# K weights loaded first, three loads on ScalarE's queue, two duplicate tiles dropped, more dummy matmuls, new instruction orders

## Chip, cores and metric

One core of one Trainium2 chip. The metric is device microseconds for one execution, lower is better. The core's engines work in parallel and each executes its own instruction list in order: TensorE (PE, matmuls and PE transposes), VectorE (DVE), ScalarE (ACT), GpSimd (POOL), and SyncE (SP), which only issues DMAs here.

## The reference, cut to what matters

```
x = A_x                                   # 1 x 2048 x 448, bf16
n = layernorm(x)
q, k, v = split(n @ A_wqkv)               # 16 heads of 28
pq, pk = phi(q), phi(k)                   # phi(t) = t+1 if t>0 else exp(t), + 1e-6
kv, z = pk^T v, sum_s pk                  # per head: linear attention
h = x + ((pq kv) / (pq z)) @ A_wo
m = layernorm(h)
out = h + (gelu(m @ B_w_gate) * (m @ B_w_up)) @ B_w_down     # 448 -> 1792 -> 448
```

## The kernel before, in words

The 2048 rows are 16 tiles of 128 rows. There are three stages, and they overlap.

Stage 1 (K stage): for each tile, VectorE takes the statistics (`bnst1`, `bnag1`: L427, L428), ScalarE makes 1/std (L434, L436), and VectorE or GpSimd writes the normalized tile `xnn` (L467, L473, L497, L500). It must be transposed to be a matmul operand. Tiles 0 to 3 are transposed on TensorE (`tr_t`, L485) and copied out of PSUM by ScalarE and VectorE (`evxA_t`, `evxD_t`: L492, L494); tiles 4 to 15 by DMA transposes (`xT`, L504). `K0 Q0 Q1 K1` are single-tile projections (L525, four matmuls each, 128 rows deep); the others work on pairs of tiles (`K2K3` and so on, L544) as two half programs `a` and `b` of 6 and 8 matmuls, each 64 rows deep, which run two at a time. phi of k is an Exp on ScalarE (`ek`, L561) and two VectorE operations (`ck`, `pk`: L562, L564). `pk` reads PSUM too, so the bank comes free after it. `pt` (L579) accumulates n^T pk over all tiles in four PSUM banks. The pairs of projections use four further banks, two at a time, so a pair waits for the `pk` of two pairs before.

Stage 2 (hinge): from the finished `pt` come z (L607, L608) and the small matrices `kv` and `w2` (L620, L636). Then tile by tile: `t1`, `dr`, `rd`, `pn` (L671, L675, L678, L680: the normalized attention weights), transposed on TensorE for tiles 0 and 1 (`tro`, L697; copies `evo`) or by a DMA for later pairs (`oT`, L708). `out` (L722 for tiles 0 and 1; L737 for pairs, halves `outa`, `outb`) gives the attention output, `hr` (L744) adds x, and the second layer norm (L427 to L440) writes `hn` (L757 on VectorE for tiles 0 and 1, L760 on GpSimd). The projections `Q4Q5` to `Q14Q15` are spread over this time. `hn` is kept twice side by side, 896 wide, so that seven 128-column transposes yield both halves in the row positions that the next stage needs. For tiles 0 and 1 GpSimd writes the second copy (`dupP_t`, L763), and TensorE transposes all seven blocks (`trh_t`, L777), which ScalarE and VectorE copy out (`evh`). Later tiles are duplicated by VectorE (`wrap`) and transposed by DMA (`hT`, L790).

Stage 3 (feed-forward): `gu` (L856 and L858, gate and up, 64 rows deep, two at a time), Gelu on ScalarE (`ge`, L881), product on VectorE (`hm`, L883), and `down` (L808, L826) in chunks of 2, 2, 4, 4 and 4 tiles; `gu2_v` is a step of the first two chunks, `gu4_v` of the last three. `outa`, `outb` of later pairs stand between them.

What sets the order: `ORDERS` is a table of task numbers for each engine, written out in advance; `_Graph.place` reads it. The waits are worked out from what tasks read and write; `HOLD` only sorts a task's waits. `LOADS` says which queue issues which input load and in what order; a string such as `sp:wqk` loads the first 384 rows of the q and k columns at once, `wqka` and `wqkb` the last 64 rows to the lower and the upper half of the partitions. The `WARM` dummy matmuls (L422) on a tile of ones come first on TensorE.

Of the kernel before, what the change touches and what calls it, by code (L numbers as in the profile page):

```python
# [7 lines left out]
ALU = mybir.AluOpType  # L8
# [36 lines left out]
)  # L45
HOLD = {
# [182 lines left out]
def bass_sequential_preLN__linear_attn_block__glu_gated_geglu__prompt_kernel(  # L229
# [14 lines left out]
    HT_SINGLE = (1,)  # L244
    B1_CHUNKS = [2, 2, 4, 4, 4]
    WARM = 40
# [4 lines left out]
    DUP_POOL = (0, 1)  # L251
    K_SINGLE = (0, 14)
    WIDE = (0, 1, 2)
    LOADS = "sp:x0 act:x1 sp:x2-3 sp:wqk sp:wqka sp:wqkb sp:x4-7 sp:x8-11 sp:x12-15"
# [4 lines left out]
    with es:  # L259
# [108 lines left out]
        def dma_w(q, name):  # L368
            kinds = "".join(k for k in "QK" if k.lower() in name[1:3])
            c0, c1 = ("Q" not in kinds) * D, (1 + ("K" in kinds)) * D  # L370
            if name[-1] in "ab":
                i = "ab".index(name[-1])
                dma(q, wqk_sb[HALF[i], 3, c0:c1], A_wqkv[384:448, c0:c1], [b_w[k][1 + i] for k in kinds], "d" + name)
            else:
                dma(q, wqk_sb[:, 0:3, c0:c1], rows3(A_wqkv, c0, c1), [b_w[k][0] for k in kinds], "d" + name)
# [48 lines left out]
        G.add("pe", warm_fn, r=[b_ones], w=[b_ps[3]], name="warm")  # L424

# [237 lines left out]
        def a2_pair(p):  # L663
# [90 lines left out]
            for t in (a, a + 1):  # L754
# [7 lines left out]
                if t in DUP_POOL:  # L762
                    op("pool", lambda e, t=t, sh=sh: e.tensor_scalar(hn[:, sh, D:2 * D], x_sb[:, t, :], mv2[:, t, 0:1], rs2[:, t:t + 1], ALU.subtract, ALU.mult),  # L763
                       [b_x[t], b_mv2[t], b_rs2[t]], [b_hnd[sh]], "dupP_%d" % t)
                elif p == 0 or p in HT_SINGLE:
# [4 lines left out]
                if p == 0:  # L770
                    banks = BK_TH[t]

                    def ftrh(e, sh=sh, banks=banks):
                        ins = None
                        for k in (0, 1, 2, 4, 5, 6, 3):
# [111 lines left out]
        for chunk, nt in enumerate(B1_CHUNKS):  # L887
# [6 lines left out]
            for t in range(t0 - t0 % 2, t0 + nt - 1, 2):  # L894
                if t < T - 2:
                    b2_pair(t)
                else:
                    b2_tile(t)
                    b2_tile(t + 1)
            t0 += nt  # L900

        G.place(ORDERS)
        G.finalize(nc, es)

# [48 lines left out]
```

## Time and profile before

| | |
|---|---|
| time, median of 3 runs | 198.53 us (197.41 to 199.61) |
| the profiled execution's own time | 200.15 us |
| its span | 198.3 us, 1.85 us less than its own time |
| TensorE matmuls busy | 187.8 us (95%) |
| VectorE, ScalarE, GpSimd busy | 126.3, 71.9, 57.7 us |
| granted TensorE clock, mean | 0.991 |

The profile is of one execution. It lists busy time by engine, the busy share in 40 slices of the span (4.96 us each), the chain of work that ended last, and the groups of instructions. The trace behind it gives each instruction with its start, its duration and, in brackets, the idle time of its engine just before it and what ended that. A "PE ... x12" row covers twelve matmuls that follow each other.

### The profile page before, as it was taken

How to read it: one execution, taken by the hardware profiler on the slowest of the kernel's cores; microseconds unless marked ns; L12 is line 12 of the kernel's file. 1: busy time of each engine (PE TensorE's matmuls, PEld its weight loads, DVE VectorE, ACT ScalarE, POOL GpSimd, SP SyncE). 2: the span in 40 equal slices, each digit the busy share in tenths (PEclk: the TensorE clock that was granted, in tenths of full speed). 3: DMA queues.
4: the chain of work that ended last, by engine and by line, in shares of the span. 5: the costliest groups of instructions: out<-in, count | busy, mean ns of one | idle time of the engine just before them, and what ended most of it. 6: DMA issues, size and time to landing. Idle time of an engine off the chain costs nothing.

```text
span 198.3 us, 4730 instructions
## 1 busy us (share of the span) xinstructions
PE 187.8 (95%) x2002; PEld 101.5 (51%) x2002; DVE 126.3 (64%) x261; ACT 71.9 (36%) x162; POOL 57.7 (29%) x105
## 2 busy tenths in 40 slices
PE   7799999999499989999999999999999999999993
PEld 7343445554158857785444444444444444444452
DVE  2669988799859975998659764564454241545231
ACT  3467634199745411331223322323223211243100
POOL 3237970154825541954223300004500000000000
PEclk9999999999969999999999999999999999999999
DMA  5982558995590092308701164010054010100003
GB/s 140 317 264 53 107 111 186 223 219 120 112 311 10 1 148 53 56 3 166 171 3 34 24 120 111 3 46 0 3 99 90 0 46 3 46 0 3 0 26 117
DMA packets 34693, 17.59 MB, mean 89 GB/s; under 512 B 27376, under 2 KB 33392, under 8 KB 34672
## 3 DMA queue, kind: packets, MB, share of 16 engines
q1 hardware_dynamic: 34528, 17.18, 38.1%
q8 instruction: 16, 0.26, 0.5%
q10 hardware_dynamic: 144, 0.11, 0.3%
q14 instruction: 5, 0.04, 0.1%
HBM read 8.37 MB, written 1.84 MB: 51 GB/s over the span
## 4 chain that ended last, share of the span: by engine, by line
PE 79%; DVE 11%; DMA 6%; issue 1%; POOL 1%; ACT 1%; SPq 0%
PE ps L858 37%; PE ps L808 17%; PE ps L737 6%; PE ps L544 5%; PE ps L579 5%; DMA wqk_sb<-in_A_wqkv_dram 3%; PE ps L525 3%; PE ps L826 3%; DVE st L427 3%; DMA pqnT<-pqn 2%; DVE hh L883 1%; DVE pk L564 1%; PE ps L856 1%; DVE e L562 1%; DVE mv L428 1%
## 5 line engine op out<-in xcount | busy, mean ns | idle before, releaser
L858 PE MATMUL ps<-hnT,wgu_sb 64*128 64x512 bf16 (+1 forms) x490 | 88.3, 333 | 0.0
L856 PE MATMUL ps<-hnT,wgu_sb 64*128 64x512 bf16 (+1 forms) x490 | 88.2, 333 | 0.0
L881 ACT ACTIVATE gl<-ps 128x256 bf16<-128x256 f32 (+1 forms) x84 | 35.2, 453 | 88.5 <-PE ps L856 86.8
L883 DVE TENSOR_TENSOR hh<-ps,gl 128x256 bf16<-128x256 f32 (+1 forms) x84 | 40.5, 507 | 39.7 <-ACT gl L881 39.7
L858 PEld LDWEIGHTS ps<-hnT,wgu_sb 64*128 64x128 bf16 x490 | 45.7, 94 | 34.1
L856 PEld LDWEIGHTS ps<-hnT,wgu_sb 64*128 64x128 bf16 x490 | 45.8, 94 | 3.0 <-issue 0.5
L808 PE MATMUL ps<-wd_sb,hh 64*128 64x448 bf16 x392 | 39.5, 349 | 0.0
L808 PEld LDWEIGHTS ps<-wd_sb,hh 64*128 64x128 bf16 x392 | 19.8, 94 | 17.6 <-issue 0.4
L671 POOL TENSOR_TENSOR t<-pq,zbc 128x448 f32<-128x448 bf16 x15 | 16.7, 1129 | 26.0 <-DVE zbc L608 10.3
L544 PE MATMUL ps<-wqk_sb,hh 64*128 64x448 bf16 x196 | 22.9, 350 | 0.5 <-DVE pk L564 0.4
L427 DVE BATCH_NORM_STATS2 st<-x_sb 128x6 f32<-128x448 bf16 x32 | 18.9, 610 | 3.6 <-DMA x_sb<-in_A_x_dram 3.5
L579 PE MATMUL ps<-pk,xnn 64*128 64x448 bf16 x128 | 14.8, 349 | 0.3 <-DVE pk L564 0.3
L544 PEld LDWEIGHTS ps<-wqk_sb,hh 64*128 64x128 bf16 x196 | 8.7, 95 | 10.2 <-PE ps L544 1.4
L813 DVE TENSOR_TENSOR x_sb<-ps,x_sb 128x896 bf16<-128x896 f32 x7 | 7.6, 1085 | 7.2 <-PE ps L808 7.2
L439 POOL TENSOR_SCALAR ln<-mv 128x2 f32<-128x2 f32 x7 | 2.0, 280 | 31.0 <-DVE mv L428 31.0
L737 PE MATMUL ps<-w2p,pqnT 64*128 64x448 bf16 x84 | 9.9, 349 | 0.9 <-DMA pqnT<-pqn 0.9
L561 ACT ACTIVATE e<-ps 128x896 bf16<-128x896 f32 (+1 forms) x10 | 7.5, 764 | 8.2 <-PE ps L544 5.5
L744 DVE TENSOR_TENSOR x_sb<-ps,x_sb 128x896 bf16<-128x896 f32 (+1 forms) x9 | 8.8, 982 | 2.3 <-PE ps L737 2.3
L760 POOL TENSOR_SCALAR hn<-x_sb,nm,rs 128x448 bf16<-128x448 bf16 x14 | 10.0, 718 | 0.6
L579 PEld LDWEIGHTS ps<-pk,xnn 64*128 64x128 bf16 x128 | 6.1, 94 | 6.7 <-DVE pk L564 1.2
L675 DVE TENSOR_REDUCE den<-t 128x32 f32<-128x896 f32 (+1 forms) x9 | 8.7, 969 | 0.4 <-POOL t L671 0.3
L564 DVE SCALAR_TENSOR_TENSOR pk<-ps,e 128x896 bf16<-128x896 f32 (+1 forms) x10 | 8.8, 892 | 0.1
(84 smaller groups left out, 153.3 us busy)
## 6 DMA issues: line engine op xcount, KB each, us to landing
wd_sb<-in_B_w_down_dram SPq DMA_DIRECT2D x1, 1568.0 KB, 7.8
out_dram<-x_sb SPq DMA_DIRECT2D x7, 224.0 KB, 2.2
x_sb<-in_A_x_dram SPq DMA_DIRECT2D x3, 448.0 KB, 7.2
wgu_sb<-in_B_w_gate_dram SPq DMA_DIRECT2D x1, 896.0 KB, 11.9
wgu_sb<-in_B_w_up_dram SPq DMA_DIRECT2D x1, 896.0 KB, 15.3
wqk_sb<-in_A_wqkv_dram SPq DMA_DIRECT2D x1, 672.0 KB, 6.5
wgu_sb<-in_B_w_gate_dram SPq DMA_DIRECT2D x1, 672.0 KB, 6.0
wgu_sb<-in_B_w_up_dram SPq DMA_DIRECT2D x1, 672.0 KB, 8.4
```

What stands on the lines that cost most here:

```text
L427: op("dve", lambda e: e.bn_stats(st[:, t, :], src_ap), [b_src], [b_st[t]], "bnst%s_%d" % (tag, t))
L544: ins = e.matmul(ps[:, bk0 + i_, 0:D], xnT[HALF[h], t, c, :], wqk_sb[HALF[h], c, c0:c0 + D], start=(part == "a" and c == 0), stop=(c == 3))
L564: op("dve", lambda e: e.scalar_tensor_tensor(pk[:, ip:ip + n, :], psK, EPS, e1[:, i:i + n, :], ALU.max, ALU.add), b_ps[bu:bu + n] + b_e1[i ...
L579: ins = e.matmul(ps[:, BK_PT[c], 0:D], xnn[HALF[h], t // 2, tcols(t, c)], pk[HALF[h], t % PK_R, :], start=(t == 0 and o == 0), stop=(t == ...
L671: op(eng, lambda e, t=t, n=n: e.tensor_tensor(t1[:, n, :], pq[:, t, :], zbc[:, :], ALU.mult), [b_pq[t]] + b_z, [b_t1[n]], "t1%s_%d" % (eng ...
L737: ins = e.matmul(ps[:, BK_OUT[n], 0:D], pqnT[rows, i2, n, g, :], w[rows, g, :], start=(g == 0 and s == 0), stop=(g == 3 and s == 1))
L760: op("pool", lambda e, t=t, sh=sh: e.tensor_scalar(hn[:, sh, 0:D], x_sb[:, t, :], nm2[:, t:t + 1], rs2[:, t:t + 1], ALU.add, ALU.mult), [b ...
L808: ins = e.matmul(ps[:, BK_O[n], 0:D], hh[HALF[h], j, (t % HR) * 128:(t % HR + 1) * 128], wd_sb[HALF[h], j, :], start=(s == 0 and j == 0), ...
L856: first = e.matmul(psG[:, jj * N:(jj + 1) * N], wgu_sb[A_, k, j * 128:(j + 1) * 128], hnT[A_, r0:r0 + nt, ka_, :], start=(k == 0), stop=(k ...
L858: ins = e.matmul(psU[:, jj * N:(jj + 1) * N], wgu_sb[B_, k, j * 128:(j + 1) * 128], hnT[B_, r0:r0 + nt, kb_, :], start=(k == 0), stop=(k = ...
L881: G.add("act", lambda e, gi=gi, cs_=cs_, psG=psG: e.activation(gl[:, gi, cs_], psG[:, cs_], AF.Gelu_apprx_tanh), r=[b_ps[BK_G[i]]], w=b_gl ...
L883: op("dve", lambda e, dst=dst, srcU=srcU, srcL=srcL: e.tensor_tensor(dst, srcU, srcL, ALU.mult), [b_ps[BK_U[i]]] + b_glh, [b_ar[j_][t % HR ...
```

## The change

Five things are changed.

- Loads. The 384 rows of q and k columns, one load of 672 KB before, become two, `wk` first and `wq` after it (336 KB each). The tails become one load that reads the 64 rows twice (`wqkt`). x of tiles 2 and 3 and the tails are issued by ScalarE instead of SyncE, ahead of its table load.
- The second copy of `hn` for tiles 0 and 1 (`dupP`, GpSimd) is left out. `trh` now makes six of its seven blocks from the one copy, and the block that wraps round from four transposes of 64 columns: 16 transposes for 14.
- 43 dummy matmuls for 40 at the start, and a new group of 7 (`fill_0`), placed after `tr_0`.
- All five orders in `ORDERS` are new, and `HOLD` with them.
- On GpSimd the constants are written in another order.

```
-    LOADS = "sp:x0 act:x1 sp:x2-3 sp:wqk sp:wqka sp:wqkb sp:x4-7 sp:x8-11 sp:x12-15"
+    LOADS = "sp:x0 act:x1 sp:wk act:x2-3 act:wqkt sp:wq sp:x4-7 sp:x8-11 sp:x12-15"
-    WARM = 40
+    WARM = 43
+    FILL = (7,)
-    DUP_POOL = (0, 1)
...
+            if name[-1] == "t":
+                src = A_wqkv[384:448, c0:c1].unsqueeze(0).to_broadcast([2, 64, c1 - c0])
+                dma(q, wqk_sb[:, 3, c0:c1], src, [b_w[k][i] for k in kinds for i in (1, 2)], "d" + name)
...
-                if t in DUP_POOL:
-                    op("pool", lambda e, t=t, sh=sh: e.tensor_scalar(hn[:, sh, D:2 * D], ...), ..., "dupP_%d" % t)
-                elif p == 0 or p in HT_SINGLE:
+                if p == 0:
+                    pass
+                elif p in HT_SINGLE:
...
-                        for k in (0, 1, 2, 4, 5, 6, 3):
+                        for k in (0, 1, 2, 4, 5, 6):
                             for h in range(2):
-                                ins = e.transpose(..., hn[HALF[h], sh, k * 128:(k + 1) * 128], ident[HALF[h], HALF[h]])
+                                c0 = k * 128 - (k > 3) * D
+                                ins = e.transpose(..., hn[HALF[h], sh, c0:c0 + 128], ident[HALF[h], HALF[h]])
+                        for r_, c0 in enumerate((384, 0)):
+                            for h in range(2):
+                                ins = e.transpose(psb[HALF[r_], banks[h], 192:256], hn[HALF[h], sh, c0:c0 + 64], ident[HALF[h], HALF[h]])
...
+        for i, n in enumerate(FILL):
+            G.add("pe", fill(n), r=[b_ones], w=[], name="fill_%d" % i)
```

In ORDERS one line of the five engines' tables, TensorE's first, shows what the rows are: numbers of tasks.

```
-    "31 38 47 55 66 63 70 85 73 88 89 81 82 97 77 98 78 83 84 79 116 80 117 93 95 94 136 96 137 121 156 123 157 124"
+    "31 38 754 66 47 55 70 63 73 85 88 77 89 81 78 82 97 79 83 98 84 80 116 117 95 93 96 136 94 137 121 156 123 157"
```

Three places show how the instructions move. In the changed file the lines stand a little lower: L422 is L425 there, L485 is L496, L525 is L536, L544 is L555, L697 is L708, L722 is L733, L737 is L748, L777 is L788 with L791, and the dummies of `fill_0` are L433.

The first place is SyncE at the program's start, the input loads; before:

```order
L355 DMA x_sb<-in_A_x_dram 128x448
L355 DMA x_sb<-in_A_x_dram 128x896
L355 DMA wqk_sb<-in_A_wqkv_dram 128x3x896
L355 DMA wqk_sb<-in_A_wqkv_dram 64x896 x2
L355 DMA x_sb<-in_A_x_dram 128x1792 x3
```

and now SyncE's first rows, followed by ScalarE's own first rows in a second piece:

```order
L355 DMA x_sb<-in_A_x_dram 128x448
L355 DMA wqk_sb<-in_A_wqkv_dram 128x3x448 x2
L355 DMA x_sb<-in_A_x_dram 128x1792 x3
L355 DMA wv_sb<-in_A_wqkv_dram 128x3x448
L355 DMA wv_sb<-in_A_wqkv_dram 64x448
```

```order
L355 DMA x_sb<-in_A_x_dram 128x448
L355 DMA x_sb<-in_A_x_dram 128x896
L355 DMA wqk_sb<-in_A_wqkv_dram 128x1x896
L414 ACT_TABLE_LOAD
L445 ACTIVATE ln<-mv,eps_t 128x1
```

The k columns have moved from behind x of tiles 2 and 3 to second place on SyncE; x of tiles 2 and 3 and the tails stand on ScalarE, ahead of its table load.

The second place is TensorE at the start: dummies, `tr`, the single projections and the first pairs; before, then now:

```order
L422 MATMUL ps<-ones_bf 128x128 x40
L485 MATMUL ps<-ident,xnn 128x64 x24
L525 MATMUL ps<-wqk_sb,hh 128x448 x4
L485 MATMUL ps<-ident,xnn 128x64 x8
L525 MATMUL ps<-wqk_sb,hh 128x448 x12
L544 MATMUL ps<-wqk_sb,hh 128x448 x14
```

```order
L425 MATMUL ps<-ones_bf 128x128 x43
L496 MATMUL ps<-ident,xnn 128x64 x8
L433 MATMUL ps<-ones_bf 128x128 x7
L536 MATMUL ps<-wqk_sb,hh 128x448 x4
L496 MATMUL ps<-ident,xnn 128x64 x16
L536 MATMUL ps<-wqk_sb,hh 128x448 x4
L496 MATMUL ps<-ident,xnn 128x64 x8
L536 MATMUL ps<-wqk_sb,hh 128x448 x8
L555 MATMUL ps<-wqk_sb,hh 128x448 x6
```

Three `tr` stood ahead of K0, now one does, with seven dummies behind it; `tr_1`, `tr_2` follow K0, and the last eight single-tile matmuls are K1 then Q1 (Q1 then K1 before).

The third place is TensorE at the hinge, from the second `tro` to the first `gu`; before, then now:

```order
L697 MATMUL ps<-ident,pqn 112x64 x8
L544 MATMUL ps<-wqk_sb,hh 128x448 x8
L722 MATMUL ps<-w,pqnT 128x448 x4
L544 MATMUL ps<-wqk_sb,hh 128x448 x6
L722 MATMUL ps<-w,pqnT 128x448 x4
L544 MATMUL ps<-wqk_sb,hh 128x448 x14
L777 MATMUL ps<-ident,hn 128x64 x14
L544 MATMUL ps<-wqk_sb,hh 128x448 x8
L737 MATMUL ps<-w,pqnT 128x448 x8
L777 MATMUL ps<-ident,hn 128x64 x14
L737 MATMUL ps<-w,pqnT 128x448 x8
L856 MATMUL ps<-hnT,wgu_sb 128x256
```

```order
L733 MATMUL ps<-w,pqnT 128x448 x4
L708 MATMUL ps<-ident,pqn 112x64 x8
L555 MATMUL ps<-wqk_sb,hh 128x448 x6
L733 MATMUL ps<-w,pqnT 128x448 x4
L555 MATMUL ps<-wqk_sb,hh 128x448 x22
L788 MATMUL ps<-ident,hn 128x64 x12
L791 MATMUL ps<-ident,hn 64x64 x4
L788 MATMUL ps<-ident,hn 128x64 x12
L791 MATMUL ps<-ident,hn 64x64 x4
L870 MATMUL ps<-hnT,wgu_sb 128x256
```

`outa_1` and `outb_1` (L737) have left the stretch ahead of the first `gu`: they now stand behind `gu2_2` and `gu2_3`. All projections stand ahead of both `trh`. On SyncE, `oT_1` is now issued after the fifth of the eight copies of `w2`, and `oT_3` ahead of `hT_2` and `hT_3`.

More of the change, by code (lines that the diff above doesn't have):

```diff
@@ L370, in dma_w @@
             c0, c1 = ("Q" not in kinds) * D, (1 + ("K" in kinds)) * D
-            if name[-1] in "ab":
+            if name[-1] == "t":
+                src = A_wqkv[384:448, c0:c1].unsqueeze(0).to_broadcast([2, 64, c1 - c0])
+                dma(q, wqk_sb[:, 3, c0:c1], src, [b_w[k][i] for k in kinds for i in (1, 2)], "d" + name)
+            elif name[-1] in "ab":
                 i = "ab".index(name[-1])
@@ L424, in bass_sequential_preLN__linear_attn_block__glu_gated_geglu__prompt_kernel, with fill, fn @@
         G.add("pe", warm_fn, r=[b_ones], w=[b_ps[3]], name="warm")
+        def fill(n):
+            def fn(e):
+                ins = None
+                for _ in range(n):
+                    ins = e.matmul(ps[:, 3, 0:128], ones_bf[:], ones_bf[:], start=True, stop=True)
+                return ins
+            return fn
         def ln_stats(t, src_ap, b_src, st, mv, b_st, b_mv, tag):
@@ L761, in a2_pair @@
                        [b_x[t], b_nm2[t], b_rs2[t]], [b_hn[sh], b_hnd[sh]], "nhP_%d" % t)
-                if t in DUP_POOL:
-                    op("pool", lambda e, t=t, sh=sh: e.tensor_scalar(hn[:, sh, D:2 * D], x_sb[:, t, :], mv2[:, t, 0:1], rs2[:, t:t + 1], ALU.subtract, ALU.mult),
-                       [b_x[t], b_mv2[t], b_rs2[t]], [b_hnd[sh]], "dupP_%d" % t)
-                elif p == 0 or p in HT_SINGLE:
+                if p == 0:
+                    pass
+                elif p in HT_SINGLE:
                     op("dve", lambda e, sh=sh: e.tensor_copy(hn[:, sh, D:2 * D], hn[:, sh, 0:D]), [b_hn[sh]], [b_hnd[sh]], "wrap1_%d" % t)
@@ L774, in ftrh @@
                         ins = None
-                        for k in (0, 1, 2, 4, 5, 6, 3):
+                        for k in (0, 1, 2, 4, 5, 6):
                             for h in range(2):
-                                ins = e.transpose(psb[:, banks[h], k * 64:(k + 1) * 64], hn[HALF[h], sh, k * 128:(k + 1) * 128], ident[HALF[h], HALF[h]])
+                                c0 = k * 128 - (k > 3) * D
+                                ins = e.transpose(psb[:, banks[h], k * 64:(k + 1) * 64], hn[HALF[h], sh, c0:c0 + 128], ident[HALF[h], HALF[h]])
+                        for r_, c0 in enumerate((384, 0)):
+                            for h in range(2):
+                                ins = e.transpose(psb[HALF[r_], banks[h], 192:256], hn[HALF[h], sh, c0:c0 + 64], ident[HALF[h], HALF[h]])
                         return ins
-                    G.add("pe", ftrh, r=[b_hn[sh], b_hnd[sh], b_ident], w=[b_ps[b] for b in banks], name="trh_%d" % t)
+                    G.add("pe", ftrh, r=[b_hn[sh], b_ident], w=[b_ps[b] for b in banks], name="trh_%d" % t)
                     for h, eng in enumerate(("act", "dve")):
```

78 rows, old and new, of tables (HOLD, ORDERS) are left out of this document.

## The prediction

> **What bounds the kernel now.** I read the chain by engine first, then busy time in chosen windows, then the instructions in order of time where TensorE is not full.
>
> ```profile
> PE 79%; DVE 11%; DMA 6%; issue 1%; POOL 1%; ACT 1%; SPq 0%
> ```
>
> ```profile
> core 0: us, PE busy (x) PEld busy (x) DVE busy (x) ACT busy (x) POOL busy (x), PEclk, DMA share, GB/s
> 14.40:24.15 9.75, 8.98 (x89) 3.76 (x89) 8.98 (x21) 6.75 (x16) 8.27 (x21) 1.00 0.41 81
> 24.15:37.70 13.55, 13.55 (x142) 6.80 (x144) 10.89 (x21) 4.91 (x8) 4.28 (x8) 1.00 0.78 158
> 50.80:54.80 4.00, 1.14 (x24) 0.51 (x22) 3.54 (x8) 3.06 (x6) 3.24 (x2) 1.00 0.63 122
> 54.80:58.20 3.40, 3.38 (x32) 1.59 (x34) 1.24 (x4) 1.28 (x2) 0.00 (x0) 0.50 1.02 337
> 58.20:72.00 13.80, 13.66 (x226) 11.60 (x222) 12.76 (x24) 6.28 (x12) 8.87 (x12) 1.00 0.32 53
> 95.00:195.00 100.00, 100.00 (x958) 48.56 (x954) 48.99 (x104) 27.01 (x71) 10.62 (x21) 1.00 0.18 39
> ```
>
> In each row the second number is TensorE's busy time and the third from the end the granted clock. TensorE is full from 95 to 195 us, and the change touches no matmul there; what it can win lies ahead, where TensorE idles or is slow (at full clock a 64-row matmul of 448 columns takes 13.55 / 142 = 0.095 us, as two run at a time): the start, the hinge (idle for 2.86 us of 50.8 to 54.8, then 3.40 us at granted clock 0.50) and a short wait near 72 us. Time won there reaches the end, because nothing behind has slack to swallow it except new waits.
>
> **Start.** The rows of TensorE and VectorE in order of time:
>
> ```profile
> 1.26 4.45 PE L422 MATMUL ps<-ones_bf 128*128 128x128 bf16 x40 [1.26 <-POOL ones_bf L388]
> ...
> 6.64 0.28 DVE L494 COPY hh<-ps 128x256 bf16<-128x256 bf16 x1
> ...
> 8.31 1.67 PE L525 MATMUL ps<-wqk_sb,hh 128*128 128x448 bf16 x4 [0.56 <-DMA wqk_sb<-in_A_wqkv_dram]
> ...
> 10.24 4.20 PE L525 MATMUL ps<-wqk_sb,hh 128*128 128x448 bf16 x12
> 10.35 0.29 DVE L494 COPY hh<-ps 128x256 bf16<-128x256 bf16 x1 [1.70 <-PE ps L485]
> ...
> 10.78 1.15 DVE L427 BATCH_NORM_STATS2 st<-x_sb 128x6 f32<-128x448 bf16 x2
> ...
> 15.05 0.42 DVE L562 TENSOR_SCALAR e<-e 128x448 bf16<-128x448 bf16 x1 [1.34 <-ACT e L561]
> ```
>
> K0 has its transposed tile at 6.92 and waits for weights until 8.31. The twelve matmuls of Q0, Q1, K1 take 4.20 us, 0.35 each. VectorE waits 1.70 us for the late `tr_3` and 1.34 us for the Exp of K1, which stands last of the four. From 14.4 to 24.15 VectorE is busy 8.98 of 9.75 us: it sets the pace there, since each `pk` frees the banks of a later pair. So only a VectorE that runs earlier makes this stage earlier.
>
> When would the K weights be there? The loads:
>
> ```profile
> 0.00:4.00 4.00, 2.74 (x26) 2.75 (x27) 0.55 (x1) 1.28 (x1) 1.82 (x12) 1.00 0.46 128
> 4.00:5.40 1.40, 1.40 (x16) 1.40 (x14) 1.33 (x5) 0.81 (x4) 0.44 (x1) 1.00 0.77 218
> 5.40:8.30 2.90, 1.49 (x27) 0.75 (x25) 2.36 (x10) 1.72 (x7) 0.89 (x4) 1.00 1.00 294
> ```
>
> ```profile
> wqk_sb<-in_A_wqkv_dram SPq DMA_DIRECT2D x1, 672.0 KB, 6.5
> ```
>
> By time these rows moved 0.51 MB by 4.0 us, 0.82 by 5.4, 1.67 by 8.3. x of tiles 0 to 3 is 0.46 MB (448 KB for four tiles), the old q and k load 0.69: that count is reached near 6.5, and K0 started at 8.31, so landing trails the count by up to 1.8 us. Now 0.80 MB stand up to `wk`, reached at 5.4, and 1.03 with the tails, at 6.1: landed at 5.4 to 7.9. K0 then starts between 6.95 and 7.9; I take 7.1. `wq` lands by 9.1 and x of tiles 4 to 7 at the same byte count as before, so between 8.9 (at the last row's rate) and the 10.78 at which it is first read.
>
> The Trainium skill (DMA: Bandwidth & Descriptors, "Issuing engines are not separate DMA queues") speaks against the move to ScalarE: both queues feed the same 16 engines, and a second issuer saves only time to issue. The trace neither shows nor excludes it, as only one load was ScalarE's. By it the order of bytes alone would help, which is how I counted.
>
> The new dummies: 43 x 0.111 (4.45 / 40) end at 6.03 for 5.71, and seven more take 0.78 us while `evx` of tile 0 copies out, up to 6.92: hidden, with at most the 0.3 us of the three on the path. ScalarE's two more issues take some 0.4 us each,
>
> ```profile
> 0.79 0.38 ACTq L355 DMA_DIRECT2D x_sb<-in_A_x_dram  x1
> ```
>
> and stand ahead of a table load and of work that waits for VectorE's first statistics in any case: nothing, and 0.8 us if that cover were gone.
>
> So VectorE: `tr_1`, `tr_2` come after K0 now, three `evx` and `ck` of tile 0 near 9.1 instead of about 10.6, right behind the 10.35 row; then statistics of tiles 4 and 5 at 9.1 to 10.8; K1 ahead of Q1 removes the 1.34 us. Sum: 1.34 + (0 to 1.7), of which I take 0.3, because the loads hold the first statistics: **1.6 us earlier**. The bounds are 0 (the loads or GpSimd's tiles, busy 8.27 of 9.75, hold everything) and 3.0 (both waits go). Should the projections run faster than 0.35 behind the dummies, that adds nothing beyond these bounds, as VectorE sets the pace.
>
> **Hinge.** From the first `hr` to the last wait ahead of `gu`:
>
> ```profile
> 48.00 0.62 DVE L744 TENSOR_TENSOR x_sb<-ps,x_sb 128x448 bf16<-128x448 f32 x1
> ...
> 48.65 0.63 DVE L427 BATCH_NORM_STATS2 st<-x_sb 128x6 f32<-128x448 bf16 x1
> ...
> 49.31 0.18 DVE L428 BATCH_NORM_AGGREGATE mv<-st 128x2 f32<-128x6 f32 x1
> ...
> 49.53 0.29 ACT L434 ACTIVATE ln<-mv,eps_t 128x1 f32<-128x1 f32 x1 [0.34 <-DVE mv L428]
> 49.86 0.20 ACT L436 ACTIVATE rs<-ln 128x1 f32<-128x1 f32 x1
> 50.09 0.40 DVE L757 TENSOR_SCALAR hn<-x_sb,mv,rs 128x448 bf16<-128x448 bf16 x1
> 50.16 3.88 POOL L763 TENSOR_SCALAR hn<-x_sb,mv,rs 128x448 bf16<-128x448 bf16 x2 [0.18 <-ACT rs L436]
> 50.28 0.92 ACT L588 ACTIVATE pq<-ps 128x896 bf16<-128x896 f32 x1 [0.22 <-PE ps L544]
> ...
> 52.22 0.38 PE L777 MATMUL ps<-ident,hn 64*128 64x64 bf16 x14 [1.41 <-DVE den L675]
> 52.43 0.92 PE L544 MATMUL ps<-wqk_sb,hh 64*128 64x448 bf16 x8
> 52.63 0.54 ACT L784 ACTIVATE hnT<-ps 128x448 bf16<-128x448 bf16 x1 [0.83 <-PE ps L777]
> ...
> 54.82 1.67 PE L737 MATMUL ps<-w,pqnT 64*128 64x448 bf16 x8 [1.47 <-DVE pq L667]
> ```
>
> GpSimd's duplicates take 1.94 us each; the first ends at 52.1, and `trh_1` starts at 52.22, although `hn` of its tile was ready at 50.49. The 1.41 us end with it (the bracket names a VectorE operation that merely ended then). The 1.47 us ahead of `outa_1` end too, since it leaves this stretch. What is late next? From the end of the second `out1`, tile 1 needs 0.62 + 0.63 + 0.18 + 0.29 + 0.20 + 0.40 = 2.3 us to its `hn`, then 0.38 for `trh` and 0.54 for the copy: 3.2 us to `gu`. TensorE has 22 projection matmuls in that time (0.095 each, 2.1 us) and two `trh` of 0.4: at least 0.3 us idle. ScalarE's copies of the projections, 0.92 each, stand ahead of `ln` and of the copy, so up to 1.8 more; and a `tro` may wait 0.6 for VectorE's copy of `w2` (as wide as the `hr` of 0.62) and the second `out1` 0.3 for its operand, both behind such work. I take 2.2 of a range of 0.3 to 3.9 against 2.86 now: **0.7 us won**, bounds 2.6 won and 1.0 lost. The two extra transposes for each `trh` cost 0.05 each at most, inside that.
>
> The half clock is the larger part: 32 matmuls in 54.8 to 58.2 took 3.4 us where full clock takes 1.7. It follows a stretch of the same length with TensorE a third busy, and did not follow the one before:
>
> ```profile
> 47.97:51.40 3.43, 2.83 (x24) 1.01 (x20) 3.27 (x9) 2.76 (x6) 3.25 (x3) 1.00 0.25 69
> 51.40:54.80 3.40, 1.13 (x22) 0.51 (x22) 2.97 (x6) 2.54 (x5) 2.64 (x2) 1.00 0.70 132
> ```
>
> With some 1.6 us idle together, a window of 3.4 is half busy, which lies between the 33% that lost the clock and the 83% that kept it, and the worst idle is broken by `trh_0`: I take it as kept, **1.7 us won** in the profiled execution, bounds 0 and 1.7.
>
> **Near 72 us.** `outa_2` waits 0.85 us for its DMA transpose.
>
> ```profile
> 72.71 0.74 PE L737 MATMUL ps<-w2p,pqnT 64*128 64x448 bf16 x6 [0.85 <-DMA pqnT<-pqn]
> ```
>
> ```profile
> hnT<-hn SPq DMA_TRANSPOSE x8, 4.1
> ```
>
> The Gelus of two `gu2` stand 1.53 us apart, and VectorE's `pn` and `hm` take this long to the next start:
>
> ```profile
> 61.44 0.60 ACT L881 ACTIVATE gl<-ps 128x512 bf16<-128x512 f32 x1 [0.93 <-PE ps L856]
> 62.97 0.60 ACT L881 ACTIVATE gl<-ps 128x512 bf16<-128x512 f32 x1 [0.93 <-PE ps L856]
> ```
>
> ```profile
> 64.20 1.09 DVE L685 TENSOR_TENSOR pqn<-pq,rd 128x896 bf16<-128x896 bf16 x1
> 65.22 0.68 DVE L883 TENSOR_TENSOR hh<-ps,gl 128x512 bf16<-128x512 f32 x1
> ```
>
> From `gu2_0` to `gu2_7` TensorE now does 7 `gu2` of 1.53, 44 matmuls of `out` and 56 of `down` at 0.095: 10.7 + 4.2 + 5.3 = 20.2 us. VectorE, from the same point to the duplicate of tile 3, has seven products of 0.6, eight operations as wide as `pn` (three `pn`, three `dr`, two `hr`) of 1.02, three statistics of 0.6 and small ones of some 2.8: 17.0 us; the transpose takes 4.1: 21.1. So the old 0.85 us goes and about 0.9 returns ahead of `gu2_7`: **0**, bounds 0.85 won and 2.5 lost, if VectorE also stalls as it does at 92% of 58.2 to 72. Behind that TensorE has more work queued than the transposes need; the end (last `down`, add, store) has the same operations, so nothing.
>
> **The sum.** 1.6 + 0.7 + 1.7 + 0 = 4.0 us off the profiled execution's 200.15 gives 196.15, its span 198.3 to 194.3. That execution is slower than all three runs shown, median 198.53. One profile cannot tell how often the clock loss comes, and runs 0.5 to 2.7 us shorter speak against its coming in all of them, so I count half of it against the median: 198.53 - 1.6 - 0.7 - 0.85 = **195.4 us**.
>
> **Rivals.**
>
> First, the loads hold the start. Then its term is 0: 198.53 - 0.7 - 0.85 = 197.0. For it: x of tiles 4 to 7 has the same bytes ahead as before. Against: the 1.34 us behind K1 are no load's. Chance 0.12.
>
> Second, the clock falls to a half in the changed hinge as well, so nothing of that term is won: 198.53 - 1.6 - 0.7 = 196.2, and if the median runs had kept full clock until now, 0.85 worse, 197.1. For it: about 1.6 us idle around two short `trh`; against: half busy is not a third. The Trainium skill (TensorE: Matmul & The Clock Gate, "Part 1: The HAM clock gate") says that a free-running window of some 3.4 us decides, so that the same idle time costs in one execution and not in the next. The trace agrees as far as one execution can: the slow stretch is 3.40 us long. By the same rule the seven dummies should bring full clock to K0; the trace has 40 dummies at 0.111 us without a speed-up. Chance 0.15.
>
> Third, the wait ahead of `gu2_7` eats the gain: VectorE reaches the duplicate of tile 3 about 2.5 us late, 195.4 + 2.5 = 197.9. Chance 0.12.
>
> Fourth, slower: narrow rows. The weights now come in rows of half the length, and twice as many. If a load takes its time by the row, `wk` takes 6.5 us as the whole did, from its issue near 1.2 to 7.7, and `wq` behind it until 14.2; Q0 then starts at 14.2 for 10.24, and x of tiles 4 to 7 waits too. That adds 4.0, less the 1.55 of the hinge: 201.0. It decides from the point where `wq` lands later than about 11.8, where the loss passes the hinge's gain. Against: x of tiles 0 and 1 has rows of this length and the first 4 us moved 0.51 MB although they begin with nothing moving. Chance 0.08.
>
> **Chances and range.** The forecast has 0.53. A measurement here can tell about 1%, so faster means below 196.5. The forecast counts as faster, the second rival half so, and a little of the first and third: 0.64. Same: the rest of those three, 0.27. Slower, above 200.5: the narrow rows and a little of the third: 0.09. The likeliest case alone spans 193.5 to 197; with the upper bounds of the start and hinge terms it reaches down to 192.8, with the third rival up to 198.8, and what lies beyond is the slower case and a little on each side.
>
> **What would show it.** Right: K0 near 7.1 us and K1's Exp ahead of Q1; `ck` of the second tile near 13.2 for 15.05; no GpSimd `hn` row of 1.94 us, and `gu2_0` near 53 with the granted clock at 1.00 through the hinge; TensorE idle under 1.5 us ahead of `gu2_7`; full from there to the end. Wrong: `wq` or x of tiles 4 to 7 awaited beyond 11 us; a clock of 0.50 behind the hinge; TensorE waiting over 3 us ahead of `gu2_7` or for the transposes of tiles 4 to 7.

## The result: slower by 5%, and the profile after

The changed kernel takes 208.84 us (median, 207.68 to 211.27), the kernel before 198.47 in the same comparison (197.41 to 199.61): ratio 1.050, 95% interval 1.042 to 1.059. I had forecast 195.4, in a range of 192.8 to 198.8. The profiled execution has a span of 207.3 us for 198.3 and an own time of 209.24.

The comparisons leave out executions over 1.5% above the fastest of the same kernel; the times of the kernel before spread so widely on some chips (196.34 to 203.18 us in one batch, of whose thirteen executions four remain) that its median there stands above what a ratio is taken against.

Starts of the same matmuls in the profiled executions, in us ("two losses mended" is the version of experiment 4 below):

| | K2K3 | `gu2_0` | `gu2_7` | last `gu` | span |
|---|---|---|---|---|---|
| before | 14.37 | 58.15 | 76.70 | 183.74 | 198.3 |
| changed | 21.84 | 61.39 | 87.41 | 193.62 | 207.3 |
| two losses mended | 14.10 | 53.67 | 75.38 | 181.85 | 195.6 |

So the change loses 7.47 us before K2K3, wins 4.23 of them back up to `gu2_0`, and loses 7.47 again up to `gu2_7` (part of that is no loss: tile pair 1's and pair 3's `out` now stand in this stretch). From there the difference stays near 9 to 11.

The page of the changed kernel shows both places: the chain by engine, TensorE's 40 slices with the granted clock, and ScalarE's DMA queue.

```profile
PE 72%; DMA 12%; DVE 6%; POOL 4%; ACT 4%; issue 1%; ACTq 0%
...
PE   7207997999989759999999999999999999999995
...
PEclk9955999999999978999999999999999999999999
...
q10 hardware_dynamic: 418, 0.57, 0.8%
```

DMA has 12% of the chain for 6%. TensorE does nothing in the third slice, and the clock is half in the third and fourth; a second dip stands in slices 14 and 15, with a lower clock in 15 and 16. The queue q10, ScalarE's, has 418 packets.

**First place, the start.** TensorE's rows, then the DMA share and GB/s (the last two numbers) in windows of the wait:

```profile
6.63 0.74 PE L536 MATMUL ps<-wqk_sb,hh 128*128 128x448 bf16 x3
16.60 0.56 PE L536 MATMUL ps<-wqk_sb,hh 128*128 128x448 bf16 x1 [9.22 <-DMA wqk_sb<-in_A_wqkv_dram]
17.62 1.68 PE L536 MATMUL ps<-wqk_sb,hh 128*128 128x448 bf16 x4
```

```profile
1.73 1.12 ACTq L355 DMA_DIRECT2D wqk_sb<-in_A_wqkv_dram  x1
```

```profile
8.00:10.00 2.00, 0.00 (x0) 0.00 (x0) 0.08 (x1) 0.00 (x0) 0.00 (x0) 1.00 1.01 336
...
13.00:14.00 1.00, 0.00 (x0) 0.00 (x0) 0.00 (x0) 0.00 (x0) 0.00 (x0) 0.50 0.12 47
14.00:15.00 1.00, 0.00 (x0) 0.00 (x0) 0.00 (x0) 0.00 (x0) 0.00 (x0) 0.50 0.13 50
```

K0's first three matmuls read `wk` and start at 6.63. The fourth reads the tails, `wqkt`, and waits 9.22 us. That load was issued at 1.73. When everything else has landed, it goes on alone at 47 to 50 GB/s, with a DMA share of 0.12 to 0.13, which is 2 engines of 16, where 336 GB/s flowed before. The clock falls to 0.50 in this idle time.

**Second place, between `gu2_0` and `gu2_7`.** TensorE's rows, SyncE's, and two windows:

```profile
61.39 0.28 PE L870 MATMUL ps<-hnT,wgu_sb 64*128 64x256 bf16 x1 [0.75 <-ACT hnT L798]
...
74.73 0.74 PE L748 MATMUL ps<-w2p,pqnT 64*128 64x448 bf16 x6 [3.62 <-DVE mv L439]
```

```profile
62.85 1.25 SPq L719 DMA_TRANSPOSE pqnT<-pqn  x1
64.14 1.87 SPq L355 DMA_DIRECT2D w2p<-w  x3
66.06 0.60 SPq L355 DMA_DIRECT2D wd_sb<-in_B_w_down_dram  x1
66.71 7.69 SPq L719 DMA_TRANSPOSE pqnT<-pqn  x2
```

```profile
72.00:74.80 2.80, 0.07 (x2) 0.10 (x4) 2.18 (x5) 0.00 (x0) 0.67 (x3) 1.00 0.99 184
76.00:78.00 2.00, 2.00 (x22) 1.71 (x20) 0.00 (x0) 0.00 (x0) 1.16 (x2) 0.50 0.00 0
```

The hinge itself is quiet: 0.75 us of idle time ahead of `gu2_0`. But `outa_2` waits 3.62 us. The bracket names VectorE's statistics, while the DMA engines are 0.99 busy. On SyncE `oT_1`, which waits for VectorE until 62.85, now stands ahead of three small loads of `w2` and the load of `wd`, 1568 KB. `wd` is issued at 66.06, with `oT_2` right behind it, whose result `outa_2` needs: `oT_2` lands 7.9 us after its issue, where `oT_1` took 3.1. After the wait the clock is 0.50. In the kernel before `wd` was issued at 52.81, and SyncE's next transfer, `oT_2`, only 15 us later:

```profile
52.81 0.58 SPq L355 DMA_DIRECT2D wd_sb<-in_B_w_down_dram  x1
68.17 1.26 SPq L708 DMA_TRANSPOSE pqnT<-pqn  x1
```

### The profile page after: what moved, and what is told of

Read it like the earlier page. It is cut to its first block, busy times and chain, and to the rows that moved or that the text cites. A ratio compares the mean times of both kernels' runs of the same rounds, so it can differ in the third digit from the quotient of the medians.

```text
span 207.3 us, 4749 instructions
## 1 busy us (share of the span) xinstructions
PE 187.3 (90%) x2016; PEld 105.7 (51%) x2016; DVE 125.2 (60%) x261; ACT 71.5 (35%) x162; POOL 54.1 (26%) x103
## 4 chain that ended last, share of the span: by engine, by line
PE 72%; DMA 12%; DVE 6%; POOL 4%; ACT 4%; issue 1%; ACTq 0%
PE ps L872 32%; PE ps L822 17%; DMA wqk_sb<-in_A_wqkv_dram 7%; PE ps L555 6%; PE ps L748 4%; PE ps L590 4%; PE ps L840 3%; DMA hh<-xnn 2%; PE ps L870 2%; DMA hnT<-hn 2%; PE ps L536 2%; POOL hn L771 1%; DVE x_sb L755 1%; POOL t L682 1%; DVE st L438 1%
## 5 line engine op out<-in xcount | busy, mean ns | idle before, releaser
L870 PE MATMUL ps<-hnT,wgu_sb 64*128 64x512 bf16 (+1 forms) x490 | 90.1, 337 | 0.9 <-ACT hnT L798 0.7
L872 PE MATMUL ps<-hnT,wgu_sb 64*128 64x512 bf16 (+1 forms) x490 | 90.2, 337 | 0.1
L682 POOL TENSOR_TENSOR t<-pq,zbc 128x448 f32<-128x448 bf16 x15 | 17.4, 1172 | 35.9 <-DVE zbc L619 13.8
L555 PE MATMUL ps<-wqk_sb,hh 64*128 64x448 bf16 x196 | 22.7, 350 | 1.7 <-DMA hh<-xnn 1.6
L555 PEld LDWEIGHTS ps<-wqk_sb,hh 64*128 64x128 bf16 x196 | 8.9, 94 | 11.5 <-DMA hh<-xnn 2.0
L748 PE MATMUL ps<-w2p,pqnT 64*128 64x448 bf16 x84 | 10.6, 362 | 3.6 <-DVE mv L439 3.6
L536 PE MATMUL ps<-wqk_sb,hh 128*128 128x448 bf16 x16 | 5.3, 472 | 9.4 <-DMA wqk_sb<-in_A_wqkv_dram 9.2
L508 POOL TENSOR_SCALAR xnn<-x_sb,nm,rs 128x448 bf16<-128x448 bf16 (+1 forms) x12 | 8.6, 720 | 2.2 <-ACT rs L447 2.2
```

What stands on the lines that cost most here:

```text
L555: ins = e.matmul(ps[:, bk0 + i_, 0:D], xnT[HALF[h], t, c, :], wqk_sb[HALF[h], c, c0:c0 + D], start=(part == "a" and c == 0), stop=(c == 3))
L682: op(eng, lambda e, t=t, n=n: e.tensor_tensor(t1[:, n, :], pq[:, t, :], zbc[:, :], ALU.mult), [b_pq[t]] + b_z, [b_t1[n]], "t1%s_%d" % (eng ...
L748: ins = e.matmul(ps[:, BK_OUT[n], 0:D], pqnT[rows, i2, n, g, :], w[rows, g, :], start=(g == 0 and s == 0), stop=(g == 3 and s == 1))
L870: first = e.matmul(psG[:, jj * N:(jj + 1) * N], wgu_sb[A_, k, j * 128:(j + 1) * 128], hnT[A_, r0:r0 + nt, ka_, :], start=(k == 0), stop=(k ...
L872: ins = e.matmul(psU[:, jj * N:(jj + 1) * N], wgu_sb[B_, k, j * 128:(j + 1) * 128], hnT[B_, r0:r0 + nt, kb_, :], start=(k == 0), stop=(k = ...
```

## Experiments

Two theories came first. **A:** the tail load uses only two DMA engines, because of its shape. **B:** the load of `wd` delays `oT_2`. Rivals: ScalarE's queue is slow in itself, narrow rows, and VectorE's statistics.

**1. The tails in two loads.** The changed kernel, and:

```
-act:wqkt
+act:wqka act:wqkb
```

> The changed kernel, with the one load of the weight tails split into two loads of 64 rows, still on ScalarE's queue; every other task in the same place. Theory shape: the load that reads 64 rows twice is moved by two of the sixteen DMA engines (between 12.5 and 16.5 us the DMA engines were 0.13 busy at 47 GB/s while TensorE waited), so two plain loads land by 8 us, the 9.2 us wait inside K0 goes, and the time falls by 8 to 10 us to 199 to 201. Rival queue: whatever ScalarE issues is moved late when SyncE's queue is full; then the tails still land near 16 us and the time stays at 207 to 210. Rival narrow rows: the half-width loads of the weights are what is slow; then K0's first matmuls would wait too, and the time stays above 205.

Measured: 201.96 us (201.01 to 203.11), ratio to the kernel before 1.026 (1.016 to 1.036); 6.9 us less than the changed kernel, and 2.4% or some 4.8 us by the two ratios, which allow for the different batches. That is less than the 8 to 10 us expected. TensorE's rows:

```profile
9.17 0.35 PE L524 MATMUL ps<-wqk_sb,hh 128*128 128x448 bf16 x1 [1.85 <-DMA wqk_sb<-in_A_wqkv_dram]
...
68.62 0.74 PE L736 MATMUL ps<-w2p,pqnT 64*128 64x448 bf16 x6 [4.13 <-issue]
```

The same bytes on the same queue land some 6.2 us after their issue, for 14.8, though not by 8 us as expected. The queue is not slow, the load was. `outa_2` waits as before, and the bracket now names no engine at all: the second loss is another.

**2. The kernel before, with the tails in one load.** On SyncE:

```
-sp:wqka sp:wqkb
+sp:wqkt
```

> The kernel before, with only its two tail loads replaced by the one load that reads the 64 rows twice, on SyncE's queue where they stood. Theory shape: K0's fourth matmul waits until 15 to 18 us, and the time rises by 6 to 9 us to 204 to 208. Rival queue (ScalarE's): no ScalarE load is touched, so 198 to 199. Rival narrow rows: the weights still come 896 wide, so 198 to 199.

Measured: 206.41 us (205.66 and 207.15, two runs), ratio 1.048 (1.028 to 1.069).

```profile
13.69 0.55 PE L516 MATMUL ps<-wqk_sb,hh 128*128 128x448 bf16 x1 [5.25 <-DMA wqk_sb<-in_A_wqkv_dram]
```

One load makes the old kernel slower by about as much as the whole change did, on the other queue. (In the changed kernel the same load cost 2.4% by the ratios; a price depends on what else holds the stage.) K0's fourth matmul was 1.3 us earlier than I had expected at the least.

**3. The tails in two loads of the same shape,** one for k, one for q (`act:wkt act:wqt`).

> The changed kernel, with the one tail load split by columns: first the k half, then the q half, each still reading its 64 rows twice, on ScalarE's queue. Theory shape: each half is moved by the same two engines, one after the other, so K0's fourth matmul goes at 8 to 11 us and Q0's fourth at 15 to 18; the time stays within 2 us of the changed kernel's. Rival queue: both halves land late together, K0's near 16 us as now.

Measured: 208.34 us in one run. The fourth matmuls of K0 and Q0:

```profile
13.80 0.56 PE L524 MATMUL ps<-wqk_sb,hh 128*128 128x448 bf16 x1 [5.99 <-DMA wqk_sb<-in_A_wqkv_dram]
...
17.13 0.55 PE L524 MATMUL ps<-wqk_sb,hh 128*128 128x448 bf16 x1 [1.00 <-DMA wqk_sb<-in_A_wqkv_dram]
```

K0's half came later than I had expected (8 to 11 us), Q0's within what I had expected (15 to 18), so the load's size alone is not its price. What fits: until about 12.5 us the two engines also carry their part of SyncE's loads, and only then do they work at 47 to 50 GB/s for the tails alone: the changed kernel's single load, 229 kB, would take 4.8 us at 48 GB/s, and it landed 4.05 us after 12.5. That sharing is read from the windows; I did not vary it. It shows on SyncE's side too: its three large loads of x took 9.1 us (median) from issue to landing in the changed kernel and 7.2 in experiment 1, and `wv` 12.3 and 8.6.

So the load's outer dimension decides: it reads the 64 rows twice, as `[2, 64, 896]`. The Trainium skill (DMA: Bandwidth & Descriptors, "Why a DMA increments its semaphore by 16 and not by 1") gives the number of engines as the largest k up to 16 that divides the slowest dimension of both access patterns: 2 here. The share of 0.13 agrees, and so do the packets: q10 has 418, of which 144 are x of tile 1 (as in the kernel before) and 144 x of tiles 2 and 3, which leaves 130: 128 rows and 2 more, where the 128 rows of tile 1 came with 16 more.

**4. Experiment 1, and `wd` ahead of `oT_1`.** On SyncE, by names of tasks:

```
 dw2_4
-oT_1
 dw2_5
 dw2_6
 dw2_7
 dwd
+oT_1
 oT_2
```

> As the kernel with two tail loads, and on SyncE the load of the down weights (1.57 MB) moved ahead of the first transposing DMA of the attention weights, oT_1, which waits for VectorE until 62.8 us in the changed kernel. Theory order: outa_2 waited 3.6 us because its transpose was issued at 66.7, right behind that load, and landed only after it; now the load is over before, the wait is under 1 us, the clock stays at 1.00 behind it, and the time is 3 to 5 us below the kernel with two tails alone, 195 to 197. Rival: outa_2 waits for VectorE's statistics, as the trace's bracket says; then nothing changes against the kernel with two tails alone.

Measured: 197.31 us (196.17 to 198.16, ten runs), 4.65 less than experiment 1. SyncE's rows, then TensorE's:

```profile
51.50 0.59 SPq L343 DMA_DIRECT2D wd_sb<-in_B_w_down_dram  x1
55.13 12.71 SPq L707 DMA_TRANSPOSE pqnT<-pqn  x3
```

```profile
53.67 0.27 PE L858 MATMUL ps<-hnT,wgu_sb 64*128 64x256 bf16 x1 [0.74 <-ACT hnT L786]
...
59.80 0.93 PE L736 MATMUL ps<-w,pqnT 64*128 64x448 bf16 x8 [1.00 <-DMA pqnT<-pqn]
...
64.38 0.73 PE L736 MATMUL ps<-w2p,pqnT 64*128 64x448 bf16 x6
```

The row at 64.38 is `outa_2`: it has no wait any more, and it starts ahead of the VectorE statistics that the bracket had named, which now run from 64.67 to 67.63. So the engine that the bracket named was not the cause. `oT_2` lands 4.3 us after its issue, for 7.9. The row at 59.80 is `outa_1`, which did not wait in the changed kernel: 1.00 us of the wait has moved there. The edit takes the three loads of `w2`, of 98 KB at the most, along with the 1568 KB of `wd`; I put the effect down to `wd` by its size and did not separate them. Against the kernel before the ratio is 0.997 (0.992 to 1.003): the two losses make up the whole of it, and no gain is shown.

**5. The changed kernel with `wd` moved alone,** the slow tail load kept.

> The changed kernel with its one tail load kept, and only wd's load moved ahead of the first DMA transpose of attention weights on SyncE. Theory (two independent losses that add): 208.84 - 4.65 = 204.2 us, K0's fourth matmul still near 16.6 us, outa_2 waiting under 1 us where it waited 3.62. Rival (the late K stage shifts all that follows, so the transpose's wait is another one here): outa_2 still waits over 2 us and the time stays above 206 us.

Measured: 206.19 us (205.43 to 206.89), on a chip where the kernel before had 201.03; ratio 1.027 (1.020 to 1.034), for 1.050 with both losses. That is 4.6 us of 198.47, as in experiment 4; the absolute time is 2 us above what I had expected, where the rival had it, but the kernel before took 2.6 longer on that chip too.

```profile
16.55 0.56 PE L524 MATMUL ps<-wqk_sb,hh 128*128 128x448 bf16 x1 [9.05 <-DMA wqk_sb<-in_A_wqkv_dram]
...
68.30 0.93 PE L736 MATMUL ps<-w,pqnT 64*128 64x448 bf16 x8 [1.28 <-DMA pqnT<-pqn]
...
72.88 0.73 PE L736 MATMUL ps<-w2p,pqnT 64*128 64x448 bf16 x6
```

The first wait stays, the second (`outa_2`, the last row) goes, with 1.28 us moved to `outa_1` as in experiment 4. Each loss comes without the other, and by the ratios they add up within the intervals.

**6. The parts that should have won.** First the kernel before without the duplicates, with the new transposes (GpSimd's `dupP_0` and `dupP_1` left out, nothing else moved):

> The kernel before, with only the second copy of tiles 0 and 1 left out and the 16-transpose program in place of the 14; all other tasks and orders as before. Theory hinge: trh_1 no longer waits 1.41 us for GpSimd's duplicate, outa_1 still waits for its transpose, so the time falls by 0.5 to 1.5 us, and by up to 1.7 more in executions where the clock is then kept: 196 to 198 against 198 to 200. Rival: outa_1's wait takes up what trh_1's wait gives (it waited 1.47 us in the same stretch), and the time is within 0.5 us of before.

Measured: 201.79 us (197.39 to 203.07, six runs), the kernel before 200.15 (196.58 to 202.84) in the same batch. Only one of the six is below 201 us, so there is no ratio, and the times neither show a gain nor exclude a small one; what this run shows is where the wait goes, in an execution of 201.04 us. TensorE's row, and two windows of the hinge:

```profile
54.44 1.67 PE L725 MATMUL ps<-w,pqnT 64*128 64x448 bf16 x8 [2.85 <-DMA pqnT<-pqn]
```

```profile
51.40:54.80 3.40, 0.55 (x8) 0.14 (x6) 2.15 (x6) 2.05 (x4) 0.00 (x0) 0.88 0.79 156
54.80:58.20 3.40, 3.40 (x34) 1.67 (x32) 1.23 (x3) 1.50 (x2) 0.21 (x1) 0.50 1.07 370
```

The 1.41 us ahead of `trh_1` are gone, and the whole idle time has moved to `outa_1`, 2.85 us, with the half clock behind it. In this execution leaving the copies out won nothing, because `gu2_0` still stood behind `outa_1`; the new order moves `outa_1` out of the way.

Then experiment 4's version with the copies put back (`+dupP_0 +dupP_1` on GpSimd ahead of `t1p_7`, the old transposes):

> The version with the tails in two loads and wd's load moved (197.31 us), with GpSimd's second copies of the first two normalized tiles put back and the transposes reading them as before. Theory (the copies held the hinge): GpSimd starts them near 50.7 us when 1/std of the first tile is there, two of 1.94 us end near 54.6, TensorE's transposes of the second tile follow, gu2_0 near 55.6 for 53.67, so 199.2 us, and 200.9 if the clock falls to a half behind the idle time. Rival (VectorE's chain to the duplicate of tile 3 sets gu2_7 in any case): gu2_0 later but gu2_7 within 0.5 us of 75.38, and 197.3 us.

Measured: 199.96 us (198.74 to 201.69); the kernel before 201.03 there, ratio 0.997 (0.992 to 1.001).

```profile
55.13 0.38 PE L776 MATMUL ps<-ident,hn 64*128 64x64 bf16 x14 [1.67 <-POOL hn L762]
```

```profile
53.67:57.00 3.33, 1.23 (x30) 1.06 (x32) 2.15 (x5) 1.80 (x4) 1.32 (x1) 1.00 1.00 312
57.00:60.00 3.00, 3.00 (x34) 2.23 (x32) 2.48 (x5) 2.01 (x3) 1.04 (x1) 0.54 1.01 239
```

`gu2_0` starts at 56.15 for 53.67, `gu2_7` at 77.98 for 75.38, and the span is 198.1 for 195.6. So in the new order the copies cost 2.5 us in the profiled execution and nothing absorbs it; the rival falls there. The time lies between the 199.2 and 200.9 expected. The two ratios, from different chips, do not tell the versions apart.

**7. The loads and the dummies.** The kernel before with K weights first (`sp:x0 act:x1 sp:wk act:x2-3 act:wqka act:wqkb sp:wq ...`):

> The kernel before with the changed loads alone (K weights first, then Q, x of tiles 2 and 3 and the tails on ScalarE's queue, the tails as two loads), orders of the other engines as before. Theory loads: the tails land near 9.2 us as in the kernel with two tails, no earlier than before (9.1), so K0 ends when it did and the time is within 0.7 us of before. Rival, my prediction's start term carried by the loads: 1 to 1.6 us faster.

Measured: 198.33 us (195.99 to 202.27, twelve runs), ratio 0.999 (0.994 to 1.004). The loads alone make no difference that shows, and a gain above 1.2 us is excluded. Experiment 4's version with the old loads:

> The same version (197.31 us) with the input loads of the kernel before: x of tiles 2 and 3, the q and k columns in one load of 672 KB and both tails on SyncE. Theory (the loads matter for the start only through K0, and VectorE sets the pace from K2K3 on, whose first matmul stood at 14.10 against 14.37): K0 near 8.3 us for 6.75, K2K3 within 0.7 us of 14.1, 197.3 to 198.0 us. Rival (the new orders need the K weights early): K2K3 over 1 us later, 198.5 us or more.

Measured: 198.03 us (197.98 to 199.54), ratio 0.987 (0.980 to 0.995) to the kernel before, whose lowest time on that chip was 199.41. K0 starts at 8.65, K2K3 at 15.73, 1.6 us later, where the rival had it; the time lies between the two forecasts. Since experiment 4 ran on another chip, the early K weights' worth in the new order stays open. This is the one version that a ratio shows ahead of the kernel before. It ran in one batch with the version with the copies put back, 199.96 us: without the copies, and with the old loads, 1.9 us less.

Experiment 4's version with `WARM = 40` and no `fill_0`:

> The changed kernel with two tail loads and the down weights ahead of oT_1 (197.3 us), and the dummy matmuls of before: 40 at the start, none between tr_0 and K0. Theory VectorE: the single projections' speed is hidden behind loads and VectorE, so 196.8 to 198.0, no difference. Rival clock: without the ten dummies the projections stay at half clock in more executions, and the time rises by 0.7 to 2 us to 198 to 199.3.

Measured: 198.5 us (197.25 to 199.4, twelve runs), ratio 1.002 (0.997 to 1.007), on yet another chip than experiment 4. The time is in the rival's range, but the ratios do not tell the two apart, and the profiled executions ran at half clock from 10 to 12 us with the added dummies (0.51) and without (0.50). And with the k tails first, two loads of 56 KB ahead of x of tiles 2 and 3:

> The changed kernel with the down weights ahead of oT_1, and the tails in four loads: the two of the k columns (56 KB each) on ScalarE ahead of x of tiles 2 and 3, the two of the q columns on SyncE behind wq. Theory loads: K0 no longer waits 1.7 us for its fourth matmul (k tails land by 6.5), VectorE's chain starts up to 1.5 us earlier, and the time falls by 0.5 to 1.5 us to 196 to 196.8. Rival: x of tiles 2 and 3 or of 4 to 7 come later by the loads put ahead, and VectorE gains nothing: 197 to 198.

Measured: 197.99 us (196.79 to 200.3, twelve runs), ratio 1.001 (0.996 to 1.005). Its K0 starts later than any other's here:

```profile
8.71 1.67 PE L524 MATMUL ps<-wqk_sb,hh 128*128 128x448 bf16 x4 [2.16 <-DVE hh L493]
```

The tails no longer hold K0, the copy of its own transposed tile does: x of tiles 2 and 3 comes later, and that copy stands behind their statistics on VectorE. One wait took the other's place.

## Why the prediction was wrong, step by step

**The step that failed first** is in the start: "1.03 with the tails, at 6.1: landed at 5.4 to 7.9". It counted bytes against the rate of all 16 engines, and so took for granted that each load is spread over all of them. The tail load landed at 16.55. The upper end of that range was a row's lag on loads of 128 rows; no row of the trace showed a load with an outer dimension of 2, and the cost of an unseen shape should have been bounded apart, at a rate far below. Even in two loads the tails came at about 9.2, not 7.9.

**The step that failed second** is "Near 72 us ... 0". It went through VectorE and the transposes' own time, and the place was right, but the load of `wd` had no term: the part on loads stopped at the input loads, although the orders of all engines had changed. Priced by its own rows, it was to be seen: in the new order it stands behind `oT_1`, which cannot start before VectorE's `pn` of that pair, and 1568 KB stand right ahead of `oT_2`. The rest of the term held: from `gu2_0` to `gu2_7` I had summed 21.1 us, and it took 21.7 with `wd` moved, 26.0 without. Mended, it was worth 4.65 us, more than the 2.5 of my third rival.

**What held.** `wk` was in time: three matmuls of K0 at 6.63, for "near 7.1". The hinge's mechanism went as worked out: no duplicates, `gu2_0` with 0.75 us of idle time ahead in the changed kernel, the clock at 1.00 there, and 53.67 for "near 53" once the two losses are mended. That these two come so close is in part luck: the start gave 0.27 us up to K2K3 instead of 1.6, and the hinge's idle time fell from 2.86 to 0.81 us (3.27 less 2.46 busy from 50.40 to 53.67), by 2.05 where I had counted 0.7. Against that, "the 1.47 us ahead of `outa_1` end too" came true only while `wd` stood in the way; mended, `outa_1` waits 1.00 us for its transpose behind `gu2_2`. So my second rival (the clock falls again) did not come in the new hinge, and it came with the copies put back. The fourth rival, narrow rows, falls: K0 does not wait for `wk`, and experiment 7 has the halved rows at 0.999.

**What was mis-sized.** The start's 1.6 us, even without the slow load. VectorE's `ck` of the second tile stands at 13.87 for 15.05 (forecast 13.2), 1.2 us won, but TensorE's K2K3 only 0.27. TensorE has no idle time from 10 to 14 us in experiment 4 and runs at a clock of 0.51 and 0.64 there; in experiment 1, at 1.00, the same work lets K2K3 start 1.6 us earlier. So "VectorE sets the pace" did not hold up to K2K3, where TensorE's own speed decided. And that gain is not carried on: the step "only a VectorE that runs earlier makes this stage earlier" left out the DMA transposes of tiles 4 to 15. In experiments 1 and 4, which share all of the start, TensorE waits for one of them:

```profile
28.06 1.00 PE L543 MATMUL ps<-wqk_sb,hh 64*128 64x448 bf16 x6 [2.04 <-DMA hh<-xnn]
```

```profile
28.64 0.74 PE L543 MATMUL ps<-wqk_sb,hh 64*128 64x448 bf16 x6 [1.53 <-DMA hh<-xnn]
```

The one had K2K3 at 12.49, the other at 14.10: of 1.6 us, 0.6 are left at this wait. Of these versions, K2K3 and `gu2_0` stand at 12.49 and 54.77 (experiment 1), 14.10 and 53.67 (experiment 4), 14.98 and 53.76 (old dummies), 15.20 and 54.89 (k tails first), 15.73 and 55.76 (old loads): in these five executions a start before about 15 brings nothing more, and a later one costs.

Stage by stage, the kernel before and then experiment 4 (TensorE's busy time is the second number, the clock the third from the end):

```profile
24.00:34.00 10.00, 9.85 (x104) 4.93 (x106) 8.26 (x17) 4.13 (x7) 4.43 (x8) 1.00 0.64 133
...
44.00:54.00 10.00, 7.89 (x90) 3.21 (x88) 9.36 (x21) 8.46 (x18) 6.66 (x4) 1.00 0.57 122
54.00:64.00 10.00, 9.18 (x137) 6.70 (x139) 7.22 (x14) 5.18 (x8) 3.77 (x5) 0.83 0.52 165
64.00:74.00 10.00, 9.15 (x137) 7.20 (x133) 8.82 (x18) 3.18 (x7) 5.62 (x9) 1.00 0.53 73
```

```profile
24.00:34.00 10.00, 8.47 (x90) 4.07 (x88) 5.78 (x11) 3.14 (x5) 3.53 (x7) 1.00 0.90 144
...
44.00:54.00 10.00, 9.01 (x117) 4.30 (x114) 9.68 (x25) 9.42 (x20) 3.74 (x4) 1.00 0.47 104
54.00:64.00 10.00, 8.90 (x148) 7.19 (x144) 8.30 (x13) 5.42 (x9) 4.31 (x5) 1.00 0.71 200
64.00:74.00 10.00, 10.00 (x137) 6.84 (x134) 9.97 (x21) 2.11 (x4) 3.95 (x7) 1.00 0.34 65
```

In idle time the new order loses 1.38 us at 24 to 34, wins 1.12 at 44 to 54, loses 0.28 at 54 to 64 and wins 0.85 at 64 to 74; the half clock's 1.7 us come on top, and the stretches not shown cancel to 0.1. That is 2.0, and the last `gu` stands 1.9 earlier, for the 4.0 that I had summed up in this execution. The span is 2.7 shorter: TensorE's last matmul also ends 1.9 earlier, so the other 0.8 lies behind it, in the last additions and stores, where I had counted nothing.

Two sums of the prediction do not come out, and neither bears on the miss: the terms of the hinge's idle time add up to 3.0 at most, not 3.9, and the start's and the hinge's upper bounds lead from 195.4 to 192.1, not to 192.8.

**Counting half of the clock loss** against the median stood on one profile. Thirteen executions of the kernel before, in the batch of experiment 4, had mean granted clocks of 0.972 to 0.991, the ten of experiment 4 0.991 to 1.00. That speaks for a loss that is commoner in the kernel before than I allowed for; it is not shown where in those executions it lies.

## What to carry to other kernels

Before a load is priced by its bytes, look at its outer dimension: it sets how many of the 16 DMA engines carry it, and a load that reads its source twice through a leading dimension of 2 got two of them. When an order changes, list every transfer on each queue with its bytes, those without an apparent part in the change too; a large one just ahead of a DMA transpose was paid here by the matmul that waited for the transpose. And a stage that starts earlier is worth only what its other supplier, here the DMA transposes, lets through.

## What the runs showed of the hardware that I had not expected

A 224 KB load took 14.8 us, at 47 to 50 GB/s once it was alone, on ScalarE's queue; on SyncE's, in the kernel before, K0's matmul waited for it until 13.69. The same bytes in two loads of 64 rows took about 6.2.

The same instructions at the start ran at different clocks in different executions. From 10 to 12 us, in experiment 1 and in experiment 4:

```profile
10.00:12.00 2.00, 2.00 (x18) 0.96 (x17) 2.00 (x8) 1.89 (x7) 0.31 (x2) 1.00 1.08 331
```

```profile
10.00:12.00 2.00, 2.00 (x14) 0.72 (x13) 2.00 (x8) 1.32 (x5) 0.28 (x2) 0.51 1.06 339
```

Eight matmuls of 448 columns took 1.69 us in the one and 2.59 in the other. In the kernel before, the windows up to 14 us show a clock of 1.00, yet its twelve matmuls of this kind took 4.20 us, 0.35 each, for 0.21 in experiment 1: at the start, go by the durations. Later stretches of about 3.4 us with TensorE busy for 1.23 of 3.33 us (the copies put back) and 0.55 of 3.40 (the kernel before without them) were followed by a clock near 0.5; one of 1.90 of 3.00 in experiment 4 was not:

```profile
57.00:60.00 3.00, 1.90 (x30) 1.39 (x32) 2.78 (x7) 1.12 (x2) 1.45 (x3) 1.00 0.82 207
```

The Trainium skill (TensorE: Matmul & The Clock Gate, "Part 1: The HAM clock gate") says that a free-running window decides; by that the same idle time would cost in one execution and not in the next. The two executions of the same start agree, as far as two can.
